# Double buffers for staged weights and loaded q and k, and two reordered groups of loads and squares, in a fused attention and MLP kernel

## The chip, the cores and the metric

The kernel runs on one core of a Trainium2 chip. The metric is the device time of one execution in microseconds (us); lower is better. Five engines work side by side, each on its own list of instructions in order: PE (matrix products and 128x128 transposes), DVE (vector work), ACT (functions such as exp, and copies out of PSUM), POOL (vector work of a second kind) and SP, which here only issues DMAs. An instruction waits on semaphores for its data and for the space it writes to, and everything behind it on its engine waits with it.

## What is computed

```python
def _attn_ref(q, k, v, proj):                    # q, k, v: 4 x 8 x 768 x 64, proj: 64 x 6
    q_bucket = np.sum((np.einsum('bhsd,dk->bhsk', q, proj) > 0) * powers, axis=-1)   # 6 sign bits
    k_bucket = np.sum((np.einsum('bhsd,dk->bhsk', k, proj) > 0) * powers, axis=-1)
    mask = q_bucket[:, :, :, None] == k_bucket[:, :, None, :]
    scores = np.where(mask, scale * np.matmul(q, k.transpose(0, 1, 3, 2)), -1000000000.0)
    attn = softmax(scores)
    return np.matmul(attn, v)

x = attn_out.transpose(0, 2, 1, 3).reshape(3072, 512)
h = x @ w_in                                     # w_in: 512 x 2048
g = np.maximum(h, 0.0) + alpha * np.minimum(h, 0.0)
out = g @ w_out                                  # w_out: 2048 x 512
```

The two weight matrices arrive as 64-bit floats; the kernel takes them as pairs of 32-bit words and makes 32-bit floats of them itself.

## The kernel before

`fast_path` has two stages. The first is the attention, the second the MLP with its two products. (`general_path`, a slower way that holds for any data, runs only if a test on the data, `verdict`, asks for it; on this data it does not run.)

**Attention.** A pair is two heads of one batch, so there are 16 pairs. Each pair is worked in two units of 384 queries, 32 units in all (loop at L873). One unit u of the loop makes the scores of unit u in three parts (`scores`, L644: per part two blocks of 128 keys, PE products into PSUM and one ACT exp each, L658), and between the parts it finishes unit u-1: `attend` (PE, product of probabilities and v, L686), `add_last` (DVE, three sums of the probabilities into `accd`, L674 to L676), `totals` (PE, sum over keys `sm` from `accd`, L698) and `divide` (DVE, from `st`, L708, to `x`, L713, then a DMA of x to a buffer `x_s` in DRAM, L714). POOL makes two sums per unit (`add_first` L667, `add_third` L670).

The same loop prepares the next pair. In the first unit of a pair PE turns q and then k of the next pair (`turn`, L614, six transposes each; ACT copies them out, L615); in the second unit it makes the sign bits (`hash_bits`). `magnitude` (L623, ACT) squares the loaded tile in place and sums the squares, for the verdict; it runs at the end of a unit, for q in the first and for k in the second unit of a pair, and the load of the pair after (`load(pi + 2, ...)`, L918) follows it. The loaded tiles `qn` and `kn` have one buffer each (L486), so such a load can begin only after the squares of the pair before have been taken.

The loop also prepares the weights, one piece of 128x512 per unit: a load into `raw` (L534, three buffers), the absolute value on ACT (`weight_abs`, L546), six steps on DVE (`weight_parts`, `weight_sum`, L552 to L582). Pieces of `w_in` are collected in groups of four in a tile `wsi`, those of `w_out` in groups of two in `wso`, one buffer each (L567, L573). When a group is full, `weight_group` makes four differences on DVE (L599) and SP writes the group to DRAM (`w_in_s` by four DMAs, L603; `w_out_s` by one, L605).

**MLP.** Each product is made by blocks of two by two with seven block products instead of eight (class `Product`): `ff1` for one of eight pairs of rows of h (tiles `f_0` to `f_7`), `ff2` for one of three pairs of rows of the output (`z_0` to `z_2`). Four batches, and in each eight ff1 and three ff2. An ff1 takes its seven weight blocks from a tile `wi` that is loaded from `w_in_s` (`load_w`, L738, two buffers), asked for two ff1 ahead (L942). All ff2 share eight tiles `wo`, loaded from `w_out_s` once, at the start of the MLP, ahead of the loop (L933 to L935). The sums of the x blocks for a batch are four POOL instructions (`sums_x`, L732); for the first batch they stand in the attention's seventeenth unit. `verdict` (L836) stands after the third ff1.

**What sets the order.** Every engine but SP works in the order in which the program is written (`tc.keep_in_program_order`). The DMA issues on SP are placed by the framework's scheduler; once placed, they too are issued in order, so an issue that waits (for a buffer, or for its data) holds all later ones.

Of the kernel before, what the change touches and what calls it, by code (L numbers as in the profile page):

```python
# [8 lines left out]
F32 = mybir.dt.float32  # L9
# [394 lines left out]
def fast_path(  # L404
# [12 lines left out]
    nc = tc.nc  # L417
    P = 128
    B, H, S, D = q.shape
    NB = proj.shape[1]  # L420
    NTOK, DM = out.shape
# [3 lines left out]
    NC = S // P  # L425
# [20 lines left out]
    pool = attn.enter_context(tc.tile_pool(name="sb", bufs=2))  # L446
# [16 lines left out]
    NI = NF // 2  # L463
    NM = 7
    w_in_s = dram.tile([NI, P, NM, 2, P], F32, name="w_in_s")
    w_out_s = dram.tile([NI, P, NM, DM // 2], F32, name="w_out_s")
# [11 lines left out]
    def load(pi, name, queue=None):  # L478
        queue = queue or nc.sync
        b, hp = pairs[pi]  # L480
        src = {"q": q, "k": k, "v": v}[name]
        if name == "v":
            t = pool.tile([P, 2, NC * D], F32, name=f"vn{pi}", tag="vn")
            queue.dma_start(t, src[b, 2 * hp : 2 * hp + 2].rearrange("h (p c) d -> p h (c d)", c=NC))
        else:
            t = pool.tile([P, NC, 2, D], F32, name=f"{name}n{pi}", tag=f"{name}n", bufs=1)  # L486
            for s in range(2):
                queue.dma_start(t[:, :, s], src[b, 2 * hp + s].rearrange("(p c) d -> p c d", c=NC))
        nat[name, pi] = t
# [19 lines left out]
    def setup_alpha():  # L509
        ps = psum.tile([P, NF], F32, name="alps", tag="mi")  # L510
        do(PE.transpose(ps, alpha16, ident[:NF, :NF]))
        do(DVE.tensor_copy(alpha, ps))
# [3 lines left out]
    wst = {}  # L516
    HW = NW // 2
# [13 lines left out]
    def load_weight(i):  # L531
        if i < NW:
            raw[i] = pool.tile([P, 512], moe_w_in.dtype, name=f"raw{i}", tag="raw", bufs=3)
            nc.sync.dma_start(raw[i], piece(i))  # L534

    def halves(i):
        words = raw[i].bitcast(U32).rearrange("p (f t) -> p f t", t=2)
        return words[:, :, 0], words[:, :, 1]
# [4 lines left out]
    def weight_abs(i):  # L543
        lo, hi = halves(i)
        wx[i] = pool.tile([P, 512], F32, name=f"wx{i}", tag="wx")
        do(ACT.activation(wx[i], hi.bitcast(F32), AF.Abs))  # L546
# [12 lines left out]
    def weight_sum(i):  # L559


        lo, hi = halves(i)
        x, r = wx[i], wr[i]
        if i < HW:
            n, m = divmod(i, 4)
            if m == 0:
                wst[n] = pool.tile([P, NM, 4, P], F32, name=f"wsi{n}", tag="wsi", bufs=1)  # L567
            slot = (0, 5, 1, 2)[m]
            dst = wst[n][:, slot].rearrange("p i f -> p (i f)")
        else:  # L570
            n, m = divmod(i - HW, 2)
            if m == 0:
                wst[HW + n] = pool.tile([P, NM, DM // 2], F32, name=f"wso{n}", tag="wso", bufs=1)  # L573
            w = wst[HW + n]
            dst = w[:, 0:4:3] if m == 0 else w[:, 1:3]
        turned = i < HW and m == 3
        do(DVE.scalar_tensor_tensor(  # L577
            r, x, -1.0 if turned else 1.0, r, op0=ALU.mult, op1=ALU.subtract if turned else ALU.add,
        ))
        if i >= HW:  # L580
            hi, r = (t.rearrange("p (a f) -> p a f", a=2) for t in (hi, r))
        do(DVE.scalar_tensor_tensor(  # L582
            dst.bitcast(U32), hi, 0x80000000, r.bitcast(U32), op0=ALU.bitwise_and, op1=ALU.bitwise_xor,
        ))
# [34 lines left out]
    def magnitude(pi, name):  # L619

        t = nat[name, pi].rearrange("p c h d -> p (c h d)")
        n = "qk".index(name)
        do(ACT.activation(t, t, AF.Square, accum_out=mags[:, n, pi : pi + 1]))  # L623

    def hash_bits(pi, half):


        if half == 0:
            bits["q", pi] = qbs[pi % 2]
            bits["k", pi] = pool.tile([P, S], BF16, name=f"kb{pi}", tag="kb")  # L630
        cols = slice(half * CW, (half + 1) * CW)
        ps = psum.tile([P, CW], F32, name=f"hs{pi}{half}", tag="mi")
        for s in range(2):
            for n, name in enumerate("kq"):
                r = D * s + 32 * n
                do(PE.matmul(ps[r : r + 32], wh[s], tr[name, pi][:, cols], start=True, stop=True))
        for s in range(2):
            r = slice(D * s + 32, D * s + D)
            do(ACT.activation(bits["q", pi][D * s : D * s + 32, cols], ps[r], AF.Sign, bias=hb[r]))

        do(ACT.activation(bits["k", pi][:, cols], ps, AF.Sign, bias=hb))
# [20 lines left out]
    def p(u, kc):  # L662
        return prob[u, kc][:, :, :CW]

    def add_first(u):
        accp[u] = pool.tile([P, 2, CW], F32, name=f"accp{u}", tag="accp")
        do(POOL.tensor_tensor(accp[u], p(u, 0), p(u, 1), op=ALU.add))  # L667

    def add_third(u):
        do(POOL.tensor_tensor(accp[u], accp[u], p(u, 2), op=ALU.add))  # L670

    def add_last(u):
        accd[u] = pool.tile([P, 2, CW], F32, name=f"accd{u}", tag="accd", bufs=1)
        do(DVE.tensor_tensor(accd[u], p(u, 3), p(u, 4), op=ALU.add))  # L674
        do(DVE.tensor_tensor(accd[u], accd[u], p(u, 5), op=ALU.add))
        do(DVE.tensor_tensor(accd[u], accd[u], accp[u], op=ALU.add))  # L676
# [18 lines left out]
    def totals(u):  # L695
        sums[u] = psum.tile([P, CW], F32, name=f"sm{u}", tag="mi")
        for s in range(2):
            do(PE.matmul(sums[u][D * s : D * s + D], ones, accd[u][:, s], start=True, stop=True))  # L698
# [18 lines left out]
    x_m, w_m, g_m, wo = {}, {}, {}, []  # L717
# [16 lines left out]
    def load_w(n):  # L734

        if n < B * NI:
            w_m[n] = mid.tile([P, NM, 2, P], F32, name=f"wi{n}", tag="wi")
            nc.sync.dma_start(w_m[n], w_in_s[n % NI])  # L738
# [115 lines left out]


    load(0, "q")
    load(0, "k", nc.scalar)
    setup()
    load(0, "v")
# [2 lines left out]
            turn(0, name, half)  # L862
    for half in range(2):
        hash_bits(0, half)
    for name in "qk":
        magnitude(0, name)
        load(1, name)
    setup_alpha()
    load(1, "v")
    for i in range(3):  # L870
        load_weight(i)
    weight_abs(0)
    for u in range(UNITS):  # L873
        pi, g = divmod(u, NCH)
        more = pi + 1 < NPAIR
        scores(u, 0)
        add_first(u)
        if u > 0:
            add_last(u - 1)
        if more:  # L880
            if g == 0:
                turn(pi + 1, "q", 0)
                turn(pi + 1, "q", 1)
            else:
                hash_bits(pi + 1, 0)
        if u > 0:
            attend(u - 1, 0)
        weight_parts(u)
        scores(u, 1)
        add_third(u)  # L890
        weight_sum(u)
        weight_group(u)
        if more:
            if g == 0:
                turn(pi + 1, "k", 0)
                turn(pi + 1, "k", 1)
            else:
                hash_bits(pi + 1, 1)
        if u > 0:
            attend(u - 1, 1)  # L900
            totals(u - 1)
            if g == 0 and 0 < pi < NPAIR - 1:
                load(pi + 1, "v")
        scores(u, 2)
        if u > 0:
            divide(u - 1)
        load_weight(u + 3)
        if u == HW:
            load_w(0)
            load_w(1)  # L910
            load_x(0)
            sums_x(0)
        if u + 1 < NW:
            weight_abs(u + 1)
        if more:
            magnitude(pi + 1, "qk"[g])
            if pi + 2 < NPAIR:
                load(pi + 2, "qk"[g])  # L918


    late = []
# [8 lines left out]
    divide(last)  # L930
    attn.close()
    late.append(ctx.enter_context(tc.tile_pool(name="late", bufs=2)))
    for i in range(NI):  # L933
        wo.append(late[0].tile([P, NM, DM // 2], F32, name=f"wo{i}", bufs=1))
        nc.sync.dma_start(wo[i], w_out_s[i])  # L935
    blocks = [(b, what, n) for b in range(B) for what, count in (("1", NI), ("2", CH)) for n in range(count)]

    for j, (b, what, n) in enumerate(blocks):
        for st in ((2, 22, 6, 3, 7) if j == 0 else (2, 22, 5, 6, 3, 7)):
            now.step(st)  # L940
        if what == "1":
            load_w(b * NI + n + 2)  # L942
        elif n == 0 and b + 1 < B:
            load_x(b + 1)
        elif n == 1 and b + 1 < B:
            sums_x(b + 1)
        if j == 2:
            verdict()
        before = now
        if j + 1 < len(blocks):  # L950
            b, what, n = blocks[j + 1]
            now = ff1(b, n) if what == "1" else ff2(b, n)
            now.step(1)
        before.step(4)
# [29 lines left out]
```

## Time and profile before

| | |
|---|---|
| three timed runs | 1050.2, 1051.76 (median), 1054.01 us |
| the profiled execution | 1051.64 us, of which the span from first to last instruction is 1049.8 us |
| attention, to the last write of x | 0 to 450.7 us of the span |
| first ff1 products to the first ff2 | 439.4 to 534.2 us |
| busy share of the span | PE 93%, DVE 58%, ACT 36%, POOL 15% |
| mean granted PE clock | 0.969 of full speed |

The spread of the three runs is 0.36% of the median. The profile is one execution; times in it are counted from the span's start. In a timeline row the first number is the start, the second the time taken by all the instructions that the row merges (x4: four of them), and a bracket at its end tells how long the engine stood idle before it and what released it. In a row of waits stand the engine, tile and line that waited, the one it waited for, the total in us, how often, and the longest.

### The profile page before, as it was taken

The numbers are of one execution on the slowest core, as the hardware profiler recorded it, in microseconds if no ns is written. First come the engines' busy times: TensorE is split into PE (matmuls) and PEld (weight loads), VectorE is DVE, ScalarE is ACT, GpSimd is POOL, SyncE is SP. The second block draws the span as 40 slices with busy tenths as digits, with TensorE's granted clock in tenths as the row PEclk, the third lists the DMA queues.
The fourth block names the chain that finished last, engine by engine and source line by source line (L and its number), as shares of the span: only waits on it lengthen the run. The fifth ranks groups of instructions, "written<-read, shape, count | busy, mean of one in ns | idle before, by whom it ended". The sixth has DMA issues, their size and how long they took to land.

```text
span 1049.8 us, 12494 instructions
## 1 busy us (share of the span) xinstructions
PE 973.1 (93%) x4741; PEld 599.8 (57%) x4741; DVE 607.4 (58%) x959; ACT 372.9 (36%) x669; POOL 159.8 (15%) x98
## 2 busy tenths in 40 slices
PE   5969969797999999958999999999999999999997
PEld 2424324343444444334578865688755788656886
DVE  2887959799999999944660046630166600466100
ACT  5756636575776776311210022210122100222000
POOL 2232312235332333300030000030000300000000
PEclk8998979898999999988999999999999999999999
DMA  6253553535444443171340012410023400122000
GB/s 170 80 172 108 146 184 116 155 102 163 143 136 136 144 164 126 51 322 71 106 130 21 31 63 93 160 46 31 21 105 106 131 21 26 58 97 71 11 31 23
DMA packets 93317, 106.82 MB, mean 102 GB/s; under 512 B 53296, under 2 KB 79936, under 8 KB 93248
## 3 DMA queue, kind: packets, MB, share of 16 engines
q1 hardware_dynamic: 91680, 105.54, 31.0%
q8 instruction: 39, 0.64, 0.2%
q10 hardware_dynamic: 1568, 0.39, 0.2%
q14 instruction: 30, 0.25, 0.1%
HBM read 78.65 MB, written 27.26 MB: 101 GB/s over the span
## 4 chain that ended last, share of the span: by engine, by line
PE 72%; DVE 18%; DMA 6%; ACT 2%; issue 1%; SPq 0%; DVEq 0%; ACTq 0%
PE av L686 7%; PE sc L653 7%; PE z_2a L756 5%; PE z_1a L756 5%; PE z_0a L756 5%; PE z_2c L756 3%; PE z_1c L756 3%; PE z_0c L756 3%; DVE accd L676 2%; PE f_2a L756 2%; PE f_3a L756 2%; DMA kn<-in_k_dram 2%; PE f_7a L756 2%; PE f_6a L756 2%; PE f_4a L756 2%; PE f_5a L756 2%
## 5 line engine op out<-in xcount | busy, mean ns | idle before, releaser
L658 ACT ACTIVATE pt<-sc 128x768 f32<-128x768 f32 x192 | 149.9, 810 | 117.9 <-PE sc L653 117.6
L653 PE MATMUL sc<-qT,kT 64*128 64x384 f32 x768 | 156.9, 486 | 0.0
L686 PE MATMUL av<-pt,vn 128*64 128x385 f32 (+1 forms) x768 | 145.0, 515 | 0.0
L667 POOL TENSOR_TENSOR accp<-pt,pt 128x768 f32<-128x768 f32 x32 | 64.0, 2000 | 261.9 <-ACT pt L658 261.9
L686 PEld LDWEIGHTS av<-pt,vn 128*64 128x64 f32 x768 | 51.3, 141 | 76.8 <-issue 76.2
L732 POOL TENSOR_TENSOR x<-x,x 128x768 f32<-128x768 f32 x16 | 31.9, 2003 | 379.1 <-DMA x<-x_s 378.4
L810 DVE TENSOR_TENSOR g<-g,g 128x384 f32<-128x384 f32 x128 | 82.5, 665 | 2.2
L653 PEld LDWEIGHTS sc<-qT,kT 64*128 64x128 f32 x768 | 69.5, 189 | 14.9 <-issue 14.9
L653 PEld LDWEIGHTS <-kb 64*128 64x128 bf16 x384 | 24.1, 93 | 79.2 <-issue 63.0
L653 PE MATMUL sc<-qb,kb 64*128 64x384 bf16 x384 | 64.4, 328 | 5.2 <-ACT pt L658 5.0
L670 POOL TENSOR_TENSOR accp<-accp,pt 128x768 f32<-128x768 f32 x32 | 61.6, 1926 | 35.1 <-ACT pt L658 34.6
L803 DVE SCALAR_TENSOR_TENSOR g<-h,alpha 128x384 f32<-128x384 f32 x32 | 21.9, 683 | 68.4 <-ACT h L795 68.4
L756 PE MATMUL z_2a<-wo,g 128*128 128x256 f32 x256 | 58.0, 379 | 0.5 <-ACT z_2u L763 0.5
L756 PE MATMUL z_0a<-wo,g 128*128 128x256 f32 x256 | 57.9, 379 | 0.0
L756 PE MATMUL z_1a<-wo,g 128*128 128x256 f32 x256 | 57.9, 379 | 0.0
L756 PEld LDWEIGHTS z_2a<-wo,g 128*128 128x128 f32 x256 | 48.6, 190 | 8.1 <-ACT z_2u L763 0.9
L756 PEld LDWEIGHTS z_0a<-wo,g 128*128 128x128 f32 x256 | 48.6, 190 | 7.5
L756 PEld LDWEIGHTS z_1a<-wo,g 128*128 128x128 f32 x256 | 48.6, 190 | 6.6
L614 PE MATMUL tp_k<-ident,kn 128*128 128x128 f32 x96 | 17.7, 334 | 34.6 <-DMA kn<-in_k_dram 34.4
L577 DVE SCALAR_TENSOR_TENSOR wr<-wx,wr 128x512 f32<-128x512 f32 x32 | 46.8, 1463 | 1.1
L553 DVE TENSOR_SCALAR wx<-wx 128x512 uint32<-128x512 uint32 x32 | 44.1, 1379 | 1.1
L676 DVE TENSOR_TENSOR accd<-accd,accp 128x768 f32<-128x768 f32 x32 | 40.5, 1267 | 3.3
(217 smaller groups left out, 1513.2 us busy)
## 6 DMA issues: line engine op xcount, KB each, us to landing
wi<-w_in_s SPq DMA_DIRECT2D x32, 896.0 KB, 4.6
raw<-in_moe_w_in_dram SPq DMA_DIRECT2D x16, 512.0 KB, 3.7
raw<-in_moe_w_out_dram SPq DMA_DIRECT2D x16, 512.0 KB, 3.6
w_in_s<-wsi SPq DMA_DIRECT2D x16, 448.0 KB, 5.3
w_out_s<-wso SPq DMA_DIRECT2D x8, 896.0 KB, 4.2
wo<-w_out_s SPq DMA_DIRECT2D x8, 896.0 KB, 11.4
qn<-in_q_dram SPq DMA_DIRECT2D x32, 192.0 KB, 3.5
vn<-in_v_dram SPq DMA_DIRECT2D x16, 384.0 KB, 4.2
```

What stands on the lines that cost most here:

```text
L553: do(DVE.tensor_scalar(x.bitcast(U32), x.bitcast(U32), 3, 0xC0000000, op0=ALU.logical_shift_left, op1=ALU.bitwise_xor,))
L577: do(DVE.scalar_tensor_tensor(r, x, -1.0 if turned else 1.0, r, op0=ALU.mult, op1=ALU.subtract if turned else ALU.add,))
L653: do(PE.matmul(sc[:, s, :CW], what["k", pi][r, ks], what["q", pi][r, qs], start=first, stop=not first,))
L658: do(ACT.activation(pt[:, :, :CW], sc[:, :, :CW], AF.Exp, scale=SCALE / DOWN))
L667: do(POOL.tensor_tensor(accp[u], p(u, 0), p(u, 1), op=ALU.add))
L670: do(POOL.tensor_tensor(accp[u], accp[u], p(u, 2), op=ALU.add))
L676: do(DVE.tensor_tensor(accd[u], accd[u], accp[u], op=ALU.add))
L686: do(PE.matmul(av[u][D * s : D * s + D, :w], nat["v", pi][:, s, kc * D : (kc + 1) * D], prob[u, kc][:, s, :w], start=(kc == 0), stop=(kc = ...
L732: do(POOL.tensor_tensor(x_m[b, to], x_m[b, a], x_m[b, c], op=ALU.subtract))
L756: do(PE.matmul(self.ps[bank], self.left(left, k), self.right(right, k), start=start and k == 0, stop=k == self.nk - 1, skip_group_check=no ...
L803: do(DVE.scalar_tensor_tensor(g_m[m, i], h, al, h, op0=ALU.mult, op1=ALU.max))
L810: do(DVE.tensor_tensor(g_m[to, i], g_m[x, i], g_m[y, i], op=op))
```

## The change

Four edits. `qn` and `kn`, and `wsi` and `wso`, get the pool's two buffers instead of one. At the start, the loads of the second pair are asked for before the first weight pieces, and the absolute value of the first piece and the squares of the first pair move behind the first two exps. The eight `wo` loads leave the place ahead of the MLP loop; each of the first eight ff1 asks for one, after its own request for a `wi`.

```diff
-            t = pool.tile([P, NC, 2, D], F32, name=f"{name}n{pi}", tag=f"{name}n", bufs=1)
+            t = pool.tile([P, NC, 2, D], F32, name=f"{name}n{pi}", tag=f"{name}n")
...
-                wst[n] = pool.tile([P, NM, 4, P], F32, name=f"wsi{n}", tag="wsi", bufs=1)
+                wst[n] = pool.tile([P, NM, 4, P], F32, name=f"wsi{n}", tag="wsi")
...
-                wst[HW + n] = pool.tile([P, NM, DM // 2], F32, name=f"wso{n}", tag="wso", bufs=1)
+                wst[HW + n] = pool.tile([P, NM, DM // 2], F32, name=f"wso{n}", tag="wso")
...
-    for name in "qk":
-        magnitude(0, name)
-        load(1, name)
     setup_alpha()
+    load(1, "q")
+    load(1, "k")
     load(1, "v")
     for i in range(3):
         load_weight(i)
-    weight_abs(0)
     for u in range(UNITS):
...
         add_first(u)
+        if u == 0:
+            weight_abs(0)
+            magnitude(0, "q")
+            magnitude(0, "k")
...
-    for i in range(NI):
-        wo.append(late[0].tile([P, NM, DM // 2], F32, name=f"wo{i}", bufs=1))
-        nc.sync.dma_start(wo[i], w_out_s[i])
...
             load_w(b * NI + n + 2)
+            if b == 0:
+                wo.append(late[0].tile([P, NM, DM // 2], F32, name=f"wo{n}", bufs=1))
+                nc.sync.dma_start(wo[n], w_out_s[n])
```

How this moves the instructions is shown at three places, one program against the other; the number behind a tile's name is its pair, piece, group or unit, then a running number.

On SP, around the write of the first weight group (`wsi0`), in the second and third pair of the attention; `kn3` is k of the fourth pair, which PE turns in the fifth unit:

```order
+L488 DMA kn3_592<-in_k_dram 128x6x64 x2
 L534 DMA raw5_476<-in_moe_w_in_dram 128x512
 L484 DMA vn2_452<-in_v_dram 128x2x384
 L714 DMA x_s_85<-x1_473 128x384
-L488 DMA qn3_481<-in_q_dram 128x6x64 x2
+L488 DMA qn4_701<-in_q_dram 128x6x64 x2
 L534 DMA raw6_587<-in_moe_w_in_dram 128x512
 L603 DMA w_in_s_83<-wsi0_239 896x1x128 x4
 L714 DMA x_s_85<-x2_584 128x384
 L722 DMA x0_0_1995<-x_s_85 128x2x384
-L488 DMA kn3_592<-in_k_dram 128x6x64 x2
+L488 DMA kn4_804<-in_k_dram 128x6x64 x2
```

The k load of a pair moves ahead of the weight group's write and of the output x of two units; in its old place now stands the load of the pair after.

On ACT, at the start of the attention, from the last sign bits of the first pair on:

```order
 L641 ACTIVATE kb0_158<-hs01_167,hb_77 128x384
+L658 ACTIVATE pt0_87<-sc0_0_192 128x2x384
+L658 ACTIVATE pt1_88<-sc0_1_198 128x2x384
+L546 ACTIVATE wx0_206<-raw0_186 128x512
 L623 ACTIVATE qn0_97,mags_80<-qn0_97 128x768
 L623 ACTIVATE kn0_100,mags_80<-kn0_100 128x768
-L546 ACTIVATE wx0_194<-raw0_188 128x512
-L658 ACTIVATE pt0_87<-sc0_0_196 128x2x384
-L658 ACTIVATE pt1_88<-sc0_1_202 128x2x384
```

The first two exps move ahead of two squares and one absolute value, which themselves stay ahead of the copies of the second pair's q.

On SP, where the MLP begins; before:

```order
L935 DMA wo5_3634<-w_out_s_84 128x1792
L935 DMA wo6_3636<-w_out_s_84 128x1792
L935 DMA wo7_3638<-w_out_s_84 128x1792
L738 DMA wi2_3662<-w_in_s_83 128x1792
L738 DMA wi3_3709<-w_in_s_83 128x1792
L738 DMA wi4_3756<-w_in_s_83 128x1792
```

and now:

```order
L944 DMA wo0_3648<-w_out_s_84 128x1792
L944 DMA wo1_3697<-w_out_s_84 128x1792
L738 DMA wi2_3646<-w_in_s_83 128x1792
L944 DMA wo2_3746<-w_out_s_84 128x1792
L944 DMA wo3_3819<-w_out_s_84 128x1792
L738 DMA wi3_3695<-w_in_s_83 128x1792
L944 DMA wo4_3868<-w_out_s_84 128x1792
L944 DMA wo5_3917<-w_out_s_84 128x1792
L944 DMA wo6_3966<-w_out_s_84 128x1792
L738 DMA wi4_3744<-w_in_s_83 128x1792
L944 DMA wo7_4015<-w_out_s_84 128x1792
```

The weights of the third ff1 (`wi2`) stood behind eight `wo` loads and now stand behind two; `wi3` follows two more, `wi4` three more. PE, DVE and POOL do the same instructions in the same order as before.

## Prediction

> **What bounds the kernel now.** I read the page first, then the waits by stretch, then the timelines around the longest waits.
>
> ```profile
> span 1049.8 us, 12494 instructions
> ```
>
> The profiled execution took 1051.64 us, so 1.84 us lie around the span. It is 0.12 us under the median of the runs shown; I make the sum against it and carry it over unchanged. About 0.3% (3 us) is what a measurement of this kernel can tell from no change.
>
> The MLP from the first ff2 on is PE alone, busy for 505.48 of 506 us at full clock:
>
> ```profile
> 534.00:1040.00 506.00, 505.48 (x2008) 381.20 (x2007) 182.05 (x308) 80.29 (x181) 23.69 (x12) 1.00 0.18 62
> ```
>
> The change does nothing there. What is left is the attention and the step into the MLP. In the attention's first half (60 to 250 us) PE waits for k loads, and DVE waits for PE; these are the waits of DVE and then of PE in that stretch, and the windows row of the second half (columns: PE, PEld, DVE, ACT, POOL busy, clock, DMA):
>
> ```profile
> DVE st L708 <- PE sm L698: 28.2, 6, 11.6
> ```
>
> ```profile
> PE tp_k L614 <- DMA kn<-in_k_dram: 25.5, 3, 10.6
> ```
>
> ```profile
> 250.00:448.00 198.00, 189.23 (x1219) 83.24 (x1220) 187.64 (x280) 125.90 (x205) 67.04 (x33) 0.99 0.39 126
> ```
>
> In the second half DVE is busy for 187.64 of 198 us, and what is missing is the short gap behind each of 280 instructions (10.4 / 280 = 0.04 us). So DVE already sets the pace there, and in the first half the k loads do, through PE. Why the k loads are late stands in SP's timeline:
>
> ```profile
> 41.99 1.24 SPq L488 DMA_DIRECT2D kn<-in_k_dram  x2
> ...
> 64.18 5.19 SPq L603 DMA_DIRECT2D w_in_s<-wsi  x4
> ...
> 74.03 1.29 SPq L488 DMA_DIRECT2D kn<-in_k_dram  x2
> ```
>
> The load at 74.03 stands behind a weight group's write, which holds SP for 5.19 us, and an x that DVE delivers late. PE's timeline shows the wait, from 69.84 on, and the starts of two `sm` of neighbouring units:
>
> ```profile
> 79.54 1.51 PE L614 MATMUL tp_k<-ident,kn 128*128 128x128 f32 x6 [9.70 <-DMA kn<-in_k_dram]
> ...
> 96.27 0.81 PE L698 MATMUL sm<-accd,ones 128*64 128x384 f32 x4
> ...
> 108.10 0.82 PE L698 MATMUL sm<-accd,ones 128*64 128x384 f32 x4
> ```
>
> **Term 1: the second buffer for q and k.** With it the load of a pair waits only for the squares of two pairs earlier. The fourth pair's k takes the slot that the third pair's has now, the one at 41.99, which is 69.84 - 41.99 = 28 us before PE wants it. The waits on k go. What is late next? Undisturbed, PE needs 108.10 - 96.27 = 11.83 us per unit, 47.3 per four. DVE's pace is read between its long waits, four units apart, with one weight group's differences between each two:
>
> ```profile
> 85.35 0.58 DVE L708 STREAM_TRANSPOSE st<-sm 128x384 f32<-128x384 f32 x1 [9.99 <-PE sm L698]
> ...
> 146.07 0.58 DVE L708 STREAM_TRANSPOSE st<-sm 128x384 f32<-128x384 f32 x1 [11.58 <-PE sm L698]
> ...
> 201.11 0.58 DVE L708 STREAM_TRANSPOSE st<-sm 128x384 f32<-128x384 f32 x1 [5.90 <-PE sm L698]
> ```
>
> From 146.07 DVE was ready again at 201.11 - 5.90 = 195.21, so 49.1 us for four units; from 85.35 to 146.07 - 11.58 = 134.49 it is the same 49.1. The six waits sum to 28.2 and these three to 27.5, so the other three, 0.7 in all, leave DVE at over 48 us of its own. That is more than PE's 47.3: once k is on time, DVE is late from the first weight group on, and stays late. Then the gain is DVE's idle time, not PE's. The new wait is PE's at `totals`, for `accd`; behind it on PE stands the third part of the scores, whose exps DVE wants only after the weight steps in between, so DVE is not held by it in turn. PE waits on k in the second half too:
>
> ```profile
> PE tp_k L614 <- DMA kn<-in_k_dram: 8.9, 5, 5.3
> ```
>
> I book these at nothing, since DVE waits for nothing there. During the longest of them POOL does the sums of the first batch, and DVE works on without a wait:
>
> ```profile
> 247.28 8.35 POOL L732 TENSOR_TENSOR x<-x,x 128x768 f32<-128x768 f32 x4
> ```
>
> That work stays as it is. Bounds of the term: 25.5 (PE's own waits alone) and 28.2 (DVE's); I take 28.2, as the later of the two engines decides.
>
> **Term 2: the start.** PE stands still for q of the second pair, whose load waits for the first pair's squares. These are ACT's rows from the first exps on, PE's wait, and DVE's:
>
> ```profile
> 16.78 1.50 ACT L658 ACTIVATE pt<-sc 128x768 f32<-128x768 f32 x2
> 20.82 1.13 ACT L615 ACTIVATE qT<-tp_q 128x384 f32<-128x384 f32 x2 [2.54 <-PE tp_q L614]
> 23.18 0.81 ACT L658 ACTIVATE pt<-sc 128x768 f32<-128x768 f32 x1 [1.24 <-PE sc L653]
> 24.78 0.81 ACT L658 ACTIVATE pt<-sc 128x768 f32<-128x768 f32 x1 [0.79 <-PE sc L653]
> 25.60 1.12 ACT L615 ACTIVATE kT<-tp_k 128x384 f32<-128x384 f32 x2
> 27.16 1.62 ACT L658 ACTIVATE pt<-sc 128x768 f32<-128x768 f32 x2 [0.44 <-PE sc L653]
> ```
>
> ```profile
> 19.91 1.51 PE L614 MATMUL tp_q<-ident,qn 128*128 128x128 f32 x6 [4.99 <-DMA qn<-in_q_dram]
> ```
>
> ```profile
> 28.00 0.96 DVE L674 TENSOR_TENSOR accd<-pt,pt 128x768 f32<-128x768 f32 x1 [5.81 <-ACT pt L658]
> ```
>
> ACT does the same work before and after, in another order, so what it can gain is its idle time: 2.54 + 1.24 + 0.79 + 0.44 = 5.0 us. The q load moves from behind the squares to behind the first v load, so it is there when PE is free at 14.9, and PE's 4.99 us go as well. Squares and absolute value still stand ahead of the copies of q, which therefore follow the exps without a gap. DVE waited 5.81 us for these exps, so it can take the 5.0. Lower bound 2.5 (only the gap ahead of the q copies), upper 5.8; I take 5.0, the sum of the gaps.
>
> **Term 3: `wo` tile by tile.** The third ff1's weights come last of nine loads. PE's rows, SP's row, the landing times of the `wo` loads, the usual landing of `wi`, and the last product that reads the first ff1's weights:
>
> ```profile
> 452.93 1.45 PE L756 MATMUL f_0a<-x,wi 128*128 128x384 f32 x4
> ...
> 473.77 2.93 PE L756 MATMUL f_2a<-x,wi 128*128 128x384 f32 x4 [12.94 <-DMA wi<-w_in_s]
> 476.50 1.51 PE L756 MATMUL f_1a<-x,wi 128*128 128x384 f32 x4
> ```
>
> ```profile
> 450.87 4.40 SPq L935 DMA_DIRECT2D wo<-w_out_s  x8
> ```
>
> ```profile
> DMA to landing us min/median/max: 5.4/11.4/16.8
> ```
>
> ```profile
> wi<-w_in_s SPq DMA_DIRECT2D x32, 896.0 KB, 4.6
> ```
>
> The first `wo` lands 5.4 us after 450.87, at 456.3; the last, issued 4.40 / 8 = 0.55 us before 455.27, lands 16.8 us later at 471.5. That is one every (471.5 - 456.3) / 7 = 2.2 us, in order. Now `wi2` can be issued when the product at 452.93 ends, at 454.4, third in line: it lands at 456.3 + 2 x 2.2 = 460.7, and no earlier than 454.4 + 4.6 = 459.0. PE wants it at 473.77 - 12.94 = 460.83. I leave 0.3 us of the 12.94. The first products after the stop take 2.93 us for four instead of 1.51, so another 1.4 goes with the stop. Sum 12.9 - 0.3 + 1.4 = 14.0. Later loads: an ff1 is seven groups of four at up to 1.45 us, 10 us in all, and its successor's weights are asked for five groups, 7 us, ahead of their use, against 4.6 for the landing; `wi4` stands behind three `wo`, but these were issued one ff1 earlier, and 3 x 2.2 = 6.6 us of transfer are through in 10. The last `wo` stands behind `wi4`, four ff1 ahead of the first ff2. The bounds of what is left of the wait are nothing and rival A's 5.5 us.
>
> **Term 4: two buffers for the weight groups.** A new group's first write could have waited for the DMA of the old; DVE's only waits in the first half are the `sm` ones above, so this was never the case, and the gain is nothing. The buffers themselves cost no instruction; cover that could go is none.
>
> **Sum.** 28.2 + 5.0 + 14.0 = 47.2; 1051.64 - 47.2 = 1004.4 us.
>
> **Rivals.**
>
> A: *The weights still come late.* If the transfers in flight share the engines instead of following in order, `wi2` lands with `wo2` and `wo3`, 2 x 2.2 = 4.4 us later, and PE restarts slowly (1.4). Against it speaks the even landing above; for it, that the forecast leaves a margin of 0.1 us. That leaves 4.4 - 0.3 = 4.1 us more than I left, and the 1.4: 1004.4 + 5.5 = 1009.9.
>
> B: *PE loses its clock waiting for DVE.* Once DVE is late, PE waits for `accd` at each weight group. After a short stop at the verdict PE starts slowly:
>
> ```profile
> 486.43 0.38 PE L844 MATMUL vd<-ident,top 128*1 128x128 f32 x2 [1.97 <-DVE top L839]
> ...
> 487.45 2.77 PE L756 MATMUL f_3a<-x,wi 128*128 128x384 f32 x4
> ```
>
> The four after that stop take 2.77 instead of 1.45 us (the row at 452.93), 1.3 more. A longer stop costs more: behind PE's 4.99 us at the start, ACT's later gaps of 1.24 + 0.79 + 0.44 = 2.5 us are PE's slowness. The attention has 12 weight groups (four of `w_in`, eight of `w_out`), so PE would lose 12 x 1.3 = 16 to 12 x 2.5 = 30 us. Its slack against DVE is (49.1 - 47.3) / 4 = 0.45 us per unit, 14 us over 31 units; the rival decides from 14 / 12 = 1.2 us per group on. 2 to 16 us come through, in the middle 9: about 1013. For it speaks the row above, against it that PE gives most of its lead back between the groups, so that its waits may be shorter. [...]
>
> C: *The loads are early, yet k is late.* SP is one list; if an x or a weight piece holds it longer than the 28 us of lead, the k waits stay and only terms 2 and 3 remain: 1051.64 - 19.0 = 1032.6. The lead of two units speaks against it.
>
> D, *slower than before*: the busier core is throttled. The place is the MLP, where PE's busy time is the stage's time. If PE fell there to its pace in the row at 487.45, each us of work would take 1.3 / 1.45 = 0.9 us more; the rival outweighs the gain once this holds for 47.2 / (506 x 0.9) = a tenth of the stage. At a fifth it costs 506 x 0.2 x 0.9 = 91 us: 1004.4 + 91 = 1095. Against it: PE already runs 505.48 of 506 us at a granted clock of 1.00, and the change adds no work; only what comes before gets busier. [...]
>
> **How the numbers follow.** Forecast 0.72; A 0.13; B 0.09; C 0.03; D 0.02; the remaining 0.01 no difference that can be told. The range reaches below by what terms 2 and 3 can still give (0.8 + 0.3) and about 2 us of spread between runs, to 1001; above it takes in A and B, to 1015; C, D and B's upper end lie outside. Faster by over 0.3%: 0.72 + 0.13 + 0.09 + 0.03 = 0.97; within 0.01; slower 0.02.
>
> **What would show it.** Right: no wait on `kn` beyond a few tenths; `st` waits for `sm` below 2 us in all after the first weight group, and instead PE waiting for `accd`; `qn` of the second pair without a PE wait, DVE's first `accd` near 23; the first `wi` wait under 1 us and `f_2a` at about 1.5 us for four; the stretch from the first ff2 to the end unchanged. Wrong: k waits of the same length (C); `sc` and `av` at twice their time in the attention (B); `f_2a` or `f_4a` waiting for `wi` (A); a clock under 1.00 in the MLP (D); or a new wait of DVE, on POOL or on a DMA, that grows where the `sm` waits vanish.

## The result, and the profile after

The changed kernel takes 999.24 us (median of 4 runs, 997.93 to 1000.19), the kernel before 1052.12 (4 runs, 1050.20 to 1054.01): a ratio of 0.9497, 95% interval 0.9476 to 0.9517. The forecast was 1004.4 with a range from 1001 on. The direction and the places were right; the gain was larger than the forecast, 52.9 us instead of 47.2, and the time lies below the range. The profiled execution took 1000.19 us, the longest of the four, so the two profiled ones differ by 51.45.

From the page: the span, the engines, and the chain that ended last.

```profile
span 998.3 us, 12489 instructions
...
PE 963.2 (96%) x4741; PEld 594.0 (60%) x4741; DVE 605.8 (61%) x959; ACT 371.0 (37%) x669; POOL 158.5 (16%) x98
...
PE 61%; DVE 35%; ACT 1%; issue 1%; DMA 1%; DVEq 0%; SPq 0%; ACTq 0%
```

Before, the chain read

```profile
PE 72%; DVE 18%; DMA 6%; ACT 2%; issue 1%; SPq 0%; DVEq 0%; ACTq 0%
```

DMA has fallen to 1%, and DVE now holds a third of the chain (35% of 998.3 us, some 349 us), most of the attention. These are all waits of PE that the trace lists between 60 and 250 us; for DVE in the same stretch it lists none:

```profile
PE sm L698 <- DVE accd L676: 3.0, 1, 3.0
PE sc L653 <- ACT pt L658: 2.3, 14, 0.2
PE tp_q L614 <- DVE st L708: 1.8, 3, 0.6
PE hs L636 <- DVE st L708: 0.4, 1, 0.4
```

No k is waited for, and the waits have turned round: PE waits for DVE. Where the time came from is read off at two marks, the first and the last `st` of DVE. First before, then after:

```profile
37.97 0.58 DVE L708 STREAM_TRANSPOSE st<-sm 128x384 f32<-128x384 f32 x1 [0.17 <-PE sm L698]
...
446.49 0.58 DVE L708 STREAM_TRANSPOSE st<-sm 128x384 f32<-128x384 f32 x1 [0.97 <-PE sm L698]
```

```profile
31.69 0.58 DVE L708 STREAM_TRANSPOSE st<-sm 128x384 f32<-128x384 f32 x1 [0.25 <-PE sm L698]
...
409.70 0.58 DVE L708 STREAM_TRANSPOSE st<-sm 128x384 f32<-128x384 f32 x1 [0.97 <-PE sm L698]
```

| stretch | forecast, us | the two profiles, us |
|---|---|---|
| start, to the first `st` | 5.0 | 37.97 - 31.69 = 6.28 |
| attention, first to last `st` | 28.2 | 36.79 - 6.28 = 30.51 |
| last `st` to the end | 14.0 | 51.45 - 36.79 = 14.66 |
| sum | 47.2 | 51.45 |

Within the attention, DVE's windows row from the first `st` to the end of the last one, before and then after (the third pair of numbers behind the length is DVE's busy time):

```profile
37.97:446.53 408.56, 366.52 (x2361) 162.00 (x2360) 361.26 (x522) 251.66 (x412) 126.61 (x64) 0.95 0.45 136
```

```profile
31.69:409.74 378.05, 362.05 (x2361) 158.60 (x2360) 359.40 (x522) 250.44 (x412) 125.23 (x64) 0.99 0.48 144
```

DVE was not busy for 408.56 - 361.26 = 47.30 us before and for 378.05 - 359.40 = 18.65 after; what is left after is mostly the gaps of 522 instructions (18.65 / 522 = 0.04 us each). So 28.65 of the 30.51 us are idle time, as forecast, and 361.26 - 359.40 = 1.86 are busy time that came out shorter.

The step into the MLP: the third ff1 starts without a wait and at full pace. SP's rows show its weights (the one `wi`) third in line, behind two `wo`, as the forecast had it.

```profile
422.59 1.45 PE L756 MATMUL f_1a<-x,wi 128*128 128x384 f32 x4
423.88 1.45 PE L756 MATMUL f_2a<-x,wi 128*128 128x384 f32 x4
```

```profile
414.08 0.80 SPq L944 DMA_DIRECT2D wo<-w_out_s  x2
417.62 0.32 SPq L738 DMA_DIRECT2D wi<-w_in_s  x1
417.98 0.92 SPq L944 DMA_DIRECT2D wo<-w_out_s  x2
```

From the first ff2 (now at 482.83) on nothing has changed; this is the row of the same length:

```profile
482.50:988.50 506.00, 505.48 (x2008) 381.04 (x2007) 182.66 (x308) 80.45 (x181) 23.70 (x12) 1.00 0.18 62
```

### The profile page after: what moved, and what is told of

It is laid out like the page before. It is cut to its first block, busy times and chain, and to the rows that moved or that the text cites. A ratio compares the mean times of both kernels' runs of the same rounds, so it can differ in the third digit from the quotient of the medians.

```text
span 998.3 us, 12489 instructions
## 1 busy us (share of the span) xinstructions
PE 963.2 (96%) x4741; PEld 594.0 (60%) x4741; DVE 605.8 (61%) x959; ACT 371.0 (37%) x669; POOL 158.5 (16%) x98
## 4 chain that ended last, share of the span: by engine, by line
PE 61%; DVE 35%; ACT 1%; issue 1%; DMA 1%; DVEq 0%; SPq 0%; ACTq 0%
PE z_2a L756 6%; PE z_1a L756 6%; PE z_0a L756 6%; DVE accd L676 5%; DVE accd L675 4%; DVE accd L674 4%; DVE wx L553 3%; PE z_1c L756 3%; PE z_0c L756 3%; PE z_2c L756 3%; DVE wr L577 2%; DVE wr L557 2%; PE f_2a L756 2%; PE f_3a L756 2%; PE f_7a L756 2%; PE f_6a L756 2%
## 5 line engine op out<-in xcount | busy, mean ns | idle before, releaser
L686 PE MATMUL av<-pt,vn 128*64 128x385 f32 (+1 forms) x768 | 138.1, 495 | 0.0
L667 POOL TENSOR_TENSOR accp<-pt,pt 128x768 f32<-128x768 f32 x32 | 62.0, 1939 | 222.5 <-ACT pt L658 185.2
L732 POOL TENSOR_TENSOR x<-x,x 128x768 f32<-128x768 f32 x16 | 31.9, 2005 | 364.0 <-DMA x<-x_s 363.4
L676 DVE TENSOR_TENSOR accd<-accd,accp 128x768 f32<-128x768 f32 x32 | 53.4, 1667 | 3.3
L675 DVE TENSOR_TENSOR accd<-accd,pt 128x768 f32<-128x768 f32 x32 | 43.7, 1364 | 3.3
L674 DVE TENSOR_TENSOR accd<-pt,pt 128x768 f32<-128x768 f32 x32 | 40.3, 1260 | 0.0
L639 ACT ACTIVATE qb<-hs,hb 32x384 bf16<-32x384 f32 x64 | 36.7, 574 | 2.2 <-PE hs L636 1.0
```

What stands on the lines that cost most here:

```text
L686: do(PE.matmul(av[u][D * s : D * s + D, :w], nat["v", pi][:, s, kc * D : (kc + 1) * D], prob[u, kc][:, s, :w], start=(kc == 0), stop=(kc = ...
L732: do(POOL.tensor_tensor(x_m[b, to], x_m[b, a], x_m[b, c], op=ALU.subtract))
```

## The experiments

Theory: once q and k are early, DVE sets the pace of the whole attention, so what returns is DVE's time, and each us of DVE's work counts. Rivals: PE's k waits count in both halves; the order of the squares carries the gain at the start; the second buffer for the weight groups gives the extra.

**e1: the second buffer for q and k alone.**

The kernel before, with

```diff
-            t = pool.tile([P, NC, 2, D], F32, name=f"{name}n{pi}", tag=f"{name}n", bufs=1)
+            t = pool.tile([P, NC, 2, D], F32, name=f"{name}n{pi}", tag=f"{name}n")
```

> This is the kernel before with the second buffer for q and k alone (the loads of the second pair leave early with it); weight groups in one buffer, squares ahead of the first exponentials, all second weights ahead of the MLP. Theory: DVE sets the pace of the attention, and the buffer returns DVE's idle time of 28.2 us plus 2.3 us that its own instructions and the gaps between them came out shorter in the profile after (30.5 from the third unit to the last); at the start the early load of q takes away a part of PE's 4.99 us, between 0 and 4, and the MLP's wait of 12.94 us for wi stays. 30.5 + 0 to 4: 1017 to 1021 from 1051.6. Rival 1, PE's waits on k count in both halves (25.5 + 8.9 = 34.4): 1013 to 1017. Rival 2, the second buffer for the weight groups gives the 2.3 us beyond the idle time: 28.2 + 0 to 4, 1019.5 to 1023.5, and the DVE waits behind a weight group's write come back in the trace. What decides between theory and rival 2 is the next run but two beside it, one_group.

Measured: 1014.83 us (5 runs, 1013.94 to 1015.70), ratio 0.9650 (0.9634 to 0.9666): 37.7 of the 52.9 us come from this buffer alone. The last `st` starts at 409.2 us, at 409.7 in the kernel after. So all that was gained up to the end of the attention is there without the other edits. The time lies below the theory's 1017 to 1021 and in rival 1's 1013 to 1017. A part of this is the start: the first `st` stands at 32.44 instead of 37.97, 5.53 us where the theory had up to 4. Whether DVE's time or PE's waits set the rest, this run doesn't tell; e5 does.

**e2: the order of the start as before.**

```diff
+    for name in "qk":
+        magnitude(0, name)
+        load(1, name)
-    load(1, "q")
-    load(1, "k")
...
+    weight_abs(0)
     for u in range(UNITS):
...
-        if u == 0:
-            weight_abs(0)
-            magnitude(0, "q")
-            magnitude(0, "k")
```

> The kernel after, with the absolute value and the squares ahead of the first exponentials again as before. Theory: what the start gained (first accd of DVE at 21.97 instead of 28.00, 6.28 us at the first st) came from ACT, whose idle gaps made 5.0 of it. With two buffers q's load does not wait for the squares, so the gaps go away in this order too, or most of them: the squares of the first pair (ACT, ahead of the exps) then move the first exps back by their own length, but the exps of DVE's first accd have the same work ahead of them on ACT in both orders. So 0 to 2 us over the kernel after, 999 to 1001. Rival: the order itself carries the gain, and all 6 us come back, 1005.

Measured: 999.46 us (997.74 to 1000.33) beside 999.24. The squares' place is worth nothing that can be told. DVE's rows at the start, first in this run, then in the kernel after:

```profile
18.76 2.19 DVE L557 SCALAR_TENSOR_TENSOR wr<-raw,wr 128x512 f32<-128x512 uint32 x1
20.98 2.06 DVE L577 SCALAR_TENSOR_TENSOR wr<-wx,wr 128x512 f32<-128x512 f32 x1
23.08 0.69 DVE L582 SCALAR_TENSOR_TENSOR wsi<-raw,wr 128x512 uint32<-128x512 uint32 x1
23.68 0.95 DVE L674 TENSOR_TENSOR accd<-pt,pt 128x768 f32<-128x768 f32 x1
```

```profile
18.54 0.69 DVE L557 SCALAR_TENSOR_TENSOR wr<-raw,wr 128x512 f32<-128x512 uint32 x1
19.27 0.69 DVE L577 SCALAR_TENSOR_TENSOR wr<-wx,wr 128x512 f32<-128x512 f32 x1
19.99 2.06 DVE L582 SCALAR_TENSOR_TENSOR wsi<-raw,wr 128x512 uint32<-128x512 uint32 x1
21.97 0.94 DVE L674 TENSOR_TENSOR accd<-pt,pt 128x768 f32<-128x768 f32 x1
```

In neither does DVE wait ahead of `accd`. With q loaded early DVE reaches the first sum late by its own list, whichever order ACT has. And the same instruction takes 0.69 us in one place and 2.06 in another.

**e3: all second weights ahead of the MLP again.**

```diff
+    for i in range(NI):
+        wo.append(late[0].tile([P, NM, DM // 2], F32, name=f"wo{i}", bufs=1))
+        nc.sync.dma_start(wo[i], w_out_s[i])
...
-            if b == 0:
-                wo.append(late[0].tile([P, NM, DM // 2], F32, name=f"wo{n}", bufs=1))
-                nc.sync.dma_start(wo[n], w_out_s[n])
```

> The kernel after, with the second product's eight weights loaded ahead of the MLP loop again. Theory: the third ff1 waits for its weights for about 13 us and starts slowly (2.93 instead of 1.5 us for four products), 14.4 us in all: 1013.6. Rival: with the attention over earlier the weights wait less, since the loads ahead of them have nothing else beside them; below 10 us, under 1009.

Measured: 1015.29 us (1013.79 to 1015.97), 16.0 over the kernel after, against 14.4 expected. PE's rows in this run, and then in e1, which has the same loads:

```profile
435.19 2.93 PE L756 MATMUL f_2a<-x,wi 128*128 128x384 f32 x4 [12.34 <-DMA wi<-w_in_s]
437.91 2.18 PE L756 MATMUL f_1a<-x,wi 128*128 128x384 f32 x4
439.92 1.45 PE L756 MATMUL f_2b<-x,wi 128*128 128x384 f32 x4
```

```profile
436.07 2.93 PE L756 MATMUL f_2a<-x,wi 128*128 128x384 f32 x4 [12.55 <-DMA wi<-w_in_s]
438.79 2.77 PE L756 MATMUL f_1a<-x,wi 128*128 128x384 f32 x4
441.35 1.73 PE L756 MATMUL f_2b<-x,wi 128*128 128x384 f32 x4
```

The wait is the one forecast. What it costs behind it differs between executions: 1.48 + 0.73 = 2.2 us over the usual 1.45 here, 1.48 + 1.32 + 0.28 = 3.1 in e1, 1.5 in the kernel before, the one row that the forecast had.

**e4: one buffer for the weight groups.**

```diff
-                wst[n] = pool.tile([P, NM, 4, P], F32, name=f"wsi{n}", tag="wsi")
+                wst[n] = pool.tile([P, NM, 4, P], F32, name=f"wsi{n}", tag="wsi", bufs=1)
...
-                wst[HW + n] = pool.tile([P, NM, DM // 2], F32, name=f"wso{n}", tag="wso")
+                wst[HW + n] = pool.tile([P, NM, DM // 2], F32, name=f"wso{n}", tag="wso", bufs=1)
```

> The kernel after, with one buffer for the weight groups instead of two. Theory: nothing waits on that buffer, no change within 1 us of the kernel after. Rival: now that DVE is never idle it reaches a new group's first write before the old group's write to memory is done; the twelve groups wait some tenths each (the write's landing is some 5 us behind its issue), 2 to 12 us slower, and the waits of DVE on a DMA stand at L577 or the first write of a group.

Measured: 999.00 us (997.02 to 999.95). No difference, and no wait of DVE on a DMA in the attention. The second buffer gives nothing even with DVE as the bound; with it falls rival 2 of e1.

**e5: one more sum on DVE per unit.**

```diff
         do(DVE.tensor_tensor(accd[u], p(u, 3), p(u, 4), op=ALU.add))
+        do(DVE.tensor_tensor(accd[u], p(u, 3), p(u, 4), op=ALU.add))
```

> The kernel after, with DVE's first sum of a unit (L674) done twice, 32 instructions more. Theory: DVE sets the pace of the whole attention, with no idle time in it, so each costs its full length and the gap behind it, 0.96 + 0.1 us, 32 x 1.06 = 34 us: 1033. Rival: PE or the exponentials set the pace in part of the units, and DVE has slack there; then 25 us or less come through, under 1024. A second rival, that PE goes cold while it waits longer for accd and adds its own loss: over 40 us.

Measured: 1032.52 us (1032.34 to 1032.99), 33.3 over the kernel after, or 33.3 / 32 = 1.04 us for each sum. The full price comes through, so DVE has no slack in the attention, and PE's waits of before, which would have had PE as the bound, are not what the gain is made of (rival 1 of e1).

**e6: POOL's two sums per unit left out.**

```diff
-        accp[u] = pool.tile([P, 2, CW], F32, name=f"accp{u}", tag="accp")
-        do(POOL.tensor_tensor(accp[u], p(u, 0), p(u, 1), op=ALU.add))
+        pass
...
-        do(POOL.tensor_tensor(accp[u], accp[u], p(u, 2), op=ALU.add))
+        accp[u] = p(u, 2)
```

> The kernel after, with POOL's two sums per unit left out, so that the exponentials of the first two key blocks are missing from the softmax's sums (a part of the computation is left out). Theory: DVE is late only because its instructions run longer beside POOL's sums (the three accd groups take 128.8 us instead of 32 x 3 x 0.96 = 92, and others besides; some 2 us per unit); without them DVE needs about 10 us per unit, PE with 11.83 decides, and of DVE's 12.1 us per unit 0.27 x 31 = 8 go: 991. Rival: the long instructions are DVE's own (their operands, or ACT beside them), and the time stays at 999.

Measured: 982.01 us (981.79 to 983.37): 17.2 under the kernel after, twice the expectation. The costliest DVE groups of the attention, mean ns behind the busy time, first in the kernel after, then here (the three sums' lines have moved up by one: L673 is L674 above, and so on):

```profile
L676 DVE TENSOR_TENSOR accd<-accd,accp 128x768 f32<-128x768 f32 x32 | 53.4, 1667 | 3.3
L675 DVE TENSOR_TENSOR accd<-accd,pt 128x768 f32<-128x768 f32 x32 | 43.7, 1364 | 3.3
L674 DVE TENSOR_TENSOR accd<-pt,pt 128x768 f32<-128x768 f32 x32 | 40.3, 1260 | 0.0
L553 DVE TENSOR_SCALAR wx<-wx 128x512 uint32<-128x512 uint32 x32 | 36.8, 1149 | 1.1
```

```profile
L674 DVE TENSOR_TENSOR accd<-accd,pt 128x768 f32<-128x768 f32 x32 | 32.1, 1003 | 3.7 <-DVE accd L673 0.5
L675 DVE TENSOR_TENSOR accd<-accd,pt 128x768 f32<-128x768 f32 x32 | 30.6, 958 | 1.1
L673 DVE TENSOR_TENSOR accd<-pt,pt 128x768 f32<-128x768 f32 x32 | 30.5, 954 | 1.5 <-ACT pt L658 1.5
...
L553 DVE TENSOR_SCALAR wx<-wx 128x512 uint32<-128x512 uint32 x32 | 13.7, 427 | 1.1
```

The same DVE instructions are 39% shorter in sum (174.2 us against 106.9) when POOL does not make its two sums per unit beside them, so they were held up by it. L676 has another second input here (`pt` in place of `accp`), but in e7, where it reads `accp` again and DVE makes it, all four of its instructions between 104 and 155 us take 0.96 us too. Not every step gives way alike: the three sums and L553 shrink as listed, L577 goes from 867 to 692 ns and L557 from 740 to 693, while the reduction L552 stays at 676 and 678 ns, though some 11 us of it lie beside POOL's instructions in the kernel after. By what way POOL holds up the one step and not the other, no run here shows.

Now PE is the bound; the chain here reads

```profile
PE 94%; ACT 4%; DMA 1%; issue 0%; DVE 0%; SPq 0%; ACTq 0%
```

The starts of `sm` tell where the 17 us lie, and what the expectation had missed:

| `sm` of unit | after, us | e6, us | gained since the mark before |
|---|---|---|---|
| 0 | 30.83 | 31.16 | |
| 14 | 197.76 | 196.50 | 1.59 |
| 17 | 240.34 | 231.95 | 7.13 |
| 28 | 373.85 | 362.12 | 3.34 |
| 31 | 408.79 | 392.17 | 4.89 |

The even pace gives only 1.6 + 3.3 (0.11 us per unit up to unit 14, 0.30 later). The rest lies in the three units around the first batch's sums (L732 on POOL), and in the last three units, where PE no longer prepares a next pair. The first batch's sums run from 210.37 us on in the kernel after; here three of the four run from 127.07 on, so this run does not part their place from the sums left out. In the last units the expectation took PE's 11.83 per unit for a floor, and PE needs 10.0 (392.17 - 362.12 = 30.05 for three).

**e7: these sums on DVE.**

```diff
-        do(POOL.tensor_tensor(accp[u], p(u, 0), p(u, 1), op=ALU.add))
+        do(DVE.tensor_tensor(accp[u], p(u, 0), p(u, 1), op=ALU.add))
...
-        do(POOL.tensor_tensor(accp[u], accp[u], p(u, 2), op=ALU.add))
+        do(DVE.tensor_tensor(accp[u], accp[u], p(u, 2), op=ALU.add))
```

> The kernel after, with POOL's two sums per unit given to DVE. Theory: POOL's sums cost DVE some 2.1 us per unit by stretching what runs beside them; done by DVE itself they cost 2 x (0.96 + 0.04) = 2.0. So the time hardly changes, at most 0.1 to 0.2 us x 31 = 3 to 6 us faster, 993 to 999. Rival: DVE's instructions come on top, as only a part of the stretch goes away with POOL's sums: 10 to 60 us slower. A second one: DVE now stands in its own order behind exps that POOL waited for before, and each unit waits some tenths: 2 to 15 us slower.

Measured: 995.31 us (993.62 to 998.57), 3.9 under the kernel after, in the theory's band. But the second rival is there as well; DVE's row between 60 and 400 us:

```profile
DVE accp L667 <- ACT pt L658: 18.5, 15, 1.3
```

Over the whole run this wait is 27.2 us. DVE stands in order behind exponentials that are not ready, with the sums behind it for which PE waits.

**e8: the verdict's transposes spread.** The reductions stay at the third ff1 (j == 2), the four transposes go one by one behind the next four ff1, and the rest of the test behind the one after.

```diff
-            verdict()
+            verdict_tops()
+        elif 3 <= j <= 6:
+            verdict_turn(j - 3)
+        elif j == 7:
+            verdict_end()
```

> The kernel after, with the four small transposes of the verdict spread over four later steps of ff1, their reductions ahead of them. Theory: the product behind them is slow (2.00 and 2.65 us for four instead of 1.45) because PE stood still for 1.97 us and did only tiny products after it; spread out, nothing waits and PE stays at its pace: 1.97 + 0.26 of waits and 0.55 + 1.20 of slowness, 4 us, 995.2. Rival: PE slows beside DVE's verdict or for the size of the transposes, wherever they stand; then only the waits go, 997, or nothing, 999.2.

Measured: 995.29 us (994.96 to 997.86), 4.0 under the kernel after. PE's rows in the kernel after, then here:

```profile
435.04 0.38 PE L844 MATMUL vd<-ident,top 128*1 128x128 f32 x2 [1.97 <-DVE top L839]
435.68 0.47 PE L844 MATMUL vd<-ident,top 128*1 128x128 f32 x2 [0.26 <-DVE row L845]
435.98 2.00 PE L756 MATMUL f_3a<-x,wi 128*128 128x384 f32 x4
437.77 2.65 PE L756 MATMUL f_2a<-x,wi 128*128 128x384 f32 x4
```

```profile
442.49 1.45 PE L756 MATMUL f_3a<-x,wi 128*128 128x384 f32 x4
443.78 0.27 PE L846 MATMUL vd<-ident,top 128*1 128x128 f32 x1
445.19 1.45 PE L756 MATMUL f_3a<-x,wi 128*128 128x384 f32 x4
```

One by one, the small transposes do not slow PE: the four products behind the first of them take 1.46 us, the next four 1.45. What was slow came behind the stop with all four in it; this run does not part the two, and not every execution is slow there (last section).

**e9 and e10: DVE's list in another order, and both edits together.** e9 is e7 with the first sum of a unit behind the three of the unit before; e10 is e9 with e8's edit.

```diff
         scores(u, 0)
-        add_first(u)
...
         if u > 0:
             add_last(u - 1)
+        add_first(u)
```

> The kernel after with POOL's two sums on DVE as in e7, and the first of them set behind the three sums of the unit before on DVE's list instead of ahead of them. Theory: in e7 DVE waits 27.2 us in its own order for the exponentials of the unit's first part, with the sums that PE waits for behind it; behind those sums the wait falls away or holds nobody. DVE's own work is then about 10.5 us per unit and 11.2 with the weight groups' sums, less than PE's 11.8, so PE decides: near the run without POOL's sums (982.0) with DVE's longer last units and the first batch's sums on top, 2 to 6 us: 984 to 988. Rival: what e7 loses is the stretch beside POOL's sums of the first batches and the slow PE behind it, not the order: 993 to 996.

> e9 with the verdict's transposes spread as in e8. Theory: the two do not meet, and the waits of 1.97 + 0.26 go in any case, the slow products of 0 to 1.8 us behind them where there were any: 2.2 to 4 us under e9. Rival: the slow spell behind the verdict only moves to another place; 2.2 us or less under e9.

Measured: e9 984.17 us (983.42 to 985.15), ratio to before 0.9359 (0.9346 to 0.9372); e10 980.48 us (979.72 to 980.75), 0.9320 (0.9307 to 0.9333). Both as the theory had it. The waits of DVE between 60 and 380 us in e9, and e10's chain:

```profile
DVE st L708 <- PE sm L698: 4.0, 9, 0.6
DVE accp L667 <- ACT pt L658: 1.4, 8, 0.2
```

```profile
PE 92%; ACT 3%; DVE 3%; DMA 1%; issue 0%; SPq 0%; ACTq 0%; DVEq 0%
```

DVE now waits for PE, which is the bound nearly from end to end. e10 beats both kernels of this study, the changed one by 18.8 us.

## Why the prediction fell short

**What bounds the kernel** was read rightly: DVE in the second half, k loads through PE in the first, and the waits turned round as foretold. DVE's waits for `sm` come to 1.5 us, PE waits for `accd`, and nowhere for k.

By the medians, the buffer for q and k (terms 1 and 2, 33.2 us) gave 37.7 in e1, and the `wo` edit (term 3, 14.0) 16.0 in e3. Behind each term now stands what the two profiles give.

**Term 1 (28.2; profiles 30.51).** The step that failed is its upper bound. It took DVE's idle time for the most that could return, as if DVE's own work were a fixed length. It is not. The four units for which the forecast read 49.1 us of DVE (146.07 to 195.21, with one wait of 0.26 in it) take 165.20 - 117.16 = 48.04 in the kernel after:

```profile
117.16 0.57 DVE L708 STREAM_TRANSPOSE st<-sm 128x384 f32<-128x384 f32 x1
...
165.20 0.58 DVE L708 STREAM_TRANSPOSE st<-sm 128x384 f32<-128x384 f32 x1
```

Over the attention the idle time came back as forecast (28.65), and DVE's busy time came out 1.86 us shorter on top. e1 has such a surplus with this buffer alone: from its first to its last `st` it takes 409.18 - 32.44 = 376.74 us, 31.78 under the kernel before. What makes the length vary is POOL: e6 shows the three sums at 0.95 to 1.00 us on the mean, the kernel after at 1.26 to 1.67, by what POOL does beside them. Counted over the timelines between the first and the last `st`, DVE's instructions exceed the shortest of their form by 79.0 us in sum before and by 77.8 after, and every one that is more than 0.2 us too long (64 before, 63 after) lies beside one of POOL's 64 instructions there. This covers 1.1 of the 1.86 us; in the rest DVE's rows overlap one another more (11.1 us against 10.4).

**Term 2 (5.0; profiles 6.28).** Its size was too small. That the late q load holds PE, and ACT through it, fits e1, where the buffer alone gives 5.53; e2 shows that the squares' move gives nothing that can be told. The size was worked out on ACT's list ("what it can gain is its idle time"), and that was no ceiling. DVE's wait of 5.81 was no upper bound either: DVE also came to that sum 0.2 us earlier (21.97 against 28.00 - 5.81 = 22.19), and 0.25 us more went in the rest of the unit.

**Term 3 (14.0; profiles 14.66).** The wait went as computed, with the weights third in line. The 1.4 us for the slow products behind the wait was one execution's figure; e3 and e1 show 2.2 and 3.1. e3's medians put the edit at 16.0 us. The last part of the miss is spread between executions: the two profiles differ by 1.4 us less than the medians' 52.9.

**Term 4 (nothing)** is shown by e4: 999.00 against 999.24.

**The rivals.** A (weights late) and C (k late) did not come, nor D: the MLP runs at 505.48 of 506 us. B came at one place only, beside the first batch's sums:

```profile
225.84 1.55 PE L698 MATMUL sm<-accd,ones 128*64 128x384 f32 x4 [3.04 <-DVE accd L676]
227.33 0.50 PE L653 MATMUL sc<-qb,kb 64*128 64x384 bf16 x2
```

PE ran at about half pace to 232 us, at a granted clock of 0.50 from 225.13 to 231.96, and no wait of DVE came of it: DVE reached its next `st` only at 231.23 and did not wait there. The forecast's "that work stays as it is" on POOL's sums of the first batch held: in both kernels four DVE steps beside them take 1.91 to 2.19 us each instead of 0.43 to 0.69. It did not say that such a stretch counts once DVE is the bound; the three units around them are where e6 gains 7.13 us.

**The range** allowed for 3.1 us below the forecast, made of terms 2 and 3 and the spread alone. It left nothing for term 1, the largest, whose bounds both ended at or under the value taken.

## What to carry to other kernels

Where a change hands the bound from one engine to another, the sum of the new bound's idle time is a good first figure but no ceiling: its instructions have no fixed length while another engine works beside it (DVE's last sum of a unit took 1.67 us on the mean beside POOL's sums, 0.96 without them), so compare the mean of one form with its shortest occurrence. An added instruction on the suspected engine (e5) settles in one run whether it is the bound, and leaving out the neighbour's work (e6) shows what the neighbour costs it. Moving work to an idle engine can cost the busy one more than doing that work itself (2.4 us per unit against 2.0 here), and an order in which the sums that others wait for stand first (e9) was worth 11 us here.

## What the runs showed of the hardware

- POOL's 64 sums (124.5 us of POOL: 158.5 - 34.0 on the pages) lengthen DVE's work by 605.8 - 530.0 = 75.8 us, 2.4 us per unit; DVE does them itself in 2 x 1.0.
- The same stop of PE at the verdict (1.97 and up to 0.26 us, with four tiny products) went with a slow spell in 7 of the 10 profiled executions that have it (2.00 to 2.77 us for the four products behind it), and was followed by full pace at once in e1, e5 and e6 (1.45). In the kernel before and in the kernel after the granted clock is then at half for one stretch of 3.41 us; the windows row of the kernel after (the third number from the end is the clock) is

```profile
436.76:440.17 3.41, 3.41 (x7) 1.76 (x6) 0.47 (x5) 0.48 (x1) 0.00 (x0) 0.50 0.04 15
```

So the outcome changes while the stop does not. Wherever the clock falls to half in the middle of these two profiled executions, it does so for 3.41, 6.83, 10.24 or 13.65 us, whole multiples of 3.41 (in the kernel before for 10.24 from 73.84 us on and for 13.65 from 131.87 on, in the kernel after for 6.83 from 225.13 on). What decides whether a stop brings such a stretch on, the runs do not show. A single execution's slow spell is thus a poor price for a stop.
